# mLSTM kernel: q and k transposed by TensorE in four tiles and scored in fp32

## The chip, the cores and the metric

The kernel runs on one core of one Trainium2 chip. A core has TensorE (matrix products, shown as PE, its loads of the stationary operand as PEld), VectorE (DVE), ScalarE (ACT), GpSimd (POOL) and SyncE (SP), which here only issues DMAs. The metric is device time in microseconds (us) of one execution; a kernel's time is the median of its runs.

## What is computed

Four batches, eight heads, 768 steps, head dimension 40, all in fp32: a gated linear attention (mLSTM) with a running maximum, then a gated layer with a causal convolution of five taps.

```python
for t in range(S):
    m_new = np.maximum(f_gate[:, :, t] + m, i_gate[:, :, t])
    f_stab = np.exp(f_gate[:, :, t] + m - m_new)
    i_stab = np.exp(i_gate[:, :, t] - m_new)
    m = m_new
    C = f_stab[:, :, None, None] * C + i_stab[:, :, None, None] * np.einsum('bhd,bhe->bhde', vt, kt)
    n = f_stab[:, :, None] * n + i_stab[:, :, None] * kt
    h_tilde = np.einsum('bhde,bhe->bhd', C, qt)
    nq = np.einsum('bhd,bhd->bh', n, qt)[:, :, None]
    denom = np.maximum(np.abs(nq), 1.0)
    y[:, :, t] = o * h_tilde / denom
...
# x is y with the heads side by side: (4, 768, 320)
gate = 1.0 / (1.0 + np.exp(-gate_pre))      # gate_pre: causal convolution of x over 5 steps
val = x @ w_val
return (gate * val @ w_out)
```

## The kernel before

Time is cut into six stretches j of 128 steps, each stretch into two chunks p of 64. A *unit* u = 4j + b is one stretch of one batch b with all eight heads; a *group* g = 2u + p is one chunk of it. There are 24 units and 48 groups. Within a group the recurrence is done as masked attention over 64 steps, with the state of the chunk before as 40 more rows of the key side.

Per group: `args` (L353, psd) makes the logarithms of the decays with one bf16 matmul, `expo` (L366, dm) takes their exponential on ScalarE, `scores` (L371, pss) multiplies k with q, `probs` (L387, pt) multiplies scores and decays on VectorE, `keyw` (L396, kw) weighs the keys on POOL, `state` (L410, pc) and `state_out` carry the state, `heads` (L435, ph) multiplies pt with the values and the state in vc. Per unit `norm`, `norm_o`, `gate_o` make x, `x_tr` (px) transposes it, and `x_copy`, `x_rest` put it into xc and x3. After each stretch the layer runs on x: `conv0`, `conv`, `conv3` (sg, pg), `sigmoid`, `val` (pf), `z_mul` and its parts, `outp` (po), `outp_st`, `out_dma`.

For `scores` q and k are needed with the 40 columns on the partitions. Before, each block of 128x320 is turned in five steps: `prep_max` (L286, ScalarE) finds each row's largest value, `prep_scale` (L290, VectorE) makes a power of two from it (scl, and cmp for undoing it), `prep_hi` (L318, POOL) writes the scaled fp16 upper half into stk, `prep_lo` (L324, VectorE) the lower half and a second copy of one half, and `prep_tr` (L340) has a DMA transpose it into tq (q) or tk (k). One score matmul with 3 x 40 = 120 rows then sums the three products of halves. Its stationary side tk also holds identity columns (`idk`), so that the same matmul leaves q itself in the state rows. The scale of k is undone in `probs`, that of q in `norm` by the lower bound of the denominator (sct; from j = 1 on made by `scale_mul` and `scale_out`, since q is loaded there with its steps in another order). k also goes from nat into kp, where chunk 0 stands in the upper and chunk 1 in the lower 64 partitions (`load_k`), by a DMA except at the very start.

Three things set the order. The start is written out by hand (L689 to L778). After it each piece of work has a due time in units of groups, from the table LAGS and the loops at its end (`at`), and is emitted in that order; a scheduler then orders each engine's instructions by simulated time. SyncE's queue, which issues nearly all DMAs, keeps the written order. One pool of five PSUM buffers of 2 KB per partition (`ps_s`, NSH = 5, tag "big") goes round among psd, pss, px, pg, pf and po: each new tile takes the buffer of the fifth before it and waits until that one has been read. Of the start: the gates of the first stretch are computed by `gates(0, P)` on VectorE, sent through DRAM by `spread_out` and `spread_in`, and come back as rows of la and ra, without which no `args` can run; `gates(P, S)` does the other five stretches.

Of the kernel before, what the change touches and what calls it, by code (L numbers as in the profile page):

```python
# [88 lines left out]
def tile_mlstm_gated_ffn(  # L89
# [65 lines left out]
    nat = [cst.tile([P, 2, BH, D], F32, name=f"nat{i}") for i in range(2)]  # L155
    kp = cst.tile([P, 2, BH, D], F32, name="kp")
# [16 lines left out]
    tk_ = [cst.tile([P, L + H * (P + L)], F16, name=f"tk{i}") for i in range(3)]  # L173
    cmp_ = [cst.tile([P, 2, B], F32, name=f"cmp{i}") for i in range(2)]
    sct = [cst.tile([P, B], F32, name=f"sct{i}") for i in range(2)]
    spg = cst.tile([P, PB, R], BF16, name="spg")
    sel_g = cst.tile([P, PB], F32, name="sel_g")
    sel_b = cst.tile([P, B], BF16, name="sel_b")
    scl = [cst.tile([P, 2, B], F32, name=f"scl{i}") for i in range(2)]
    amx = [cst.tile([P, 2, B], F32, name=f"amx{i}") for i in range(2)]  # L180
    stk = [cst.tile([P, 2, H, P], F16, name=f"stk{i}") for i in range(2)]


    def load_qk(j, x, b0, b1):
        ts = slice(j * P, (j + 1) * P)
        if x == 1 or j == 0:
            hs = slice(b0 * H, b1 * H)
            nc.sync.dma_start(nat[j % 2][:, x, hs], (qv, kv)[x][ts, hs])
            return
        dst = nat[j % 2][:, 0].rearrange("p (h r) d -> p h (r d)", r=R)  # L190
        for b in range(b0, b1):
            nc.sync.dma_start(dst[b * PB : (b + 1) * PB], q[b, :, ts].rearrange("h (g r) d -> g h (r d)", r=R))

    def load_k(j, p, i):
        hs = slice(i * BH // 2, (i + 1) * BH // 2)
        put = nc.scalar.copy if j == i == 0 else nc.vector.tensor_copy if j < T["kpe"] else nc.sync.dma_start
        put(kp[TOK[p] : TOK[p] + L, p, hs], nat[j % 2][p * L : (p + 1) * L, 1, hs])
# [80 lines left out]
    MASKE = 0x7F800000  # L278

    def part(j, x, i):  # L280
        src = nat[j % 2][:, x]
# [4 lines left out]
    def prep_max(j, i, x):  # L286
        junk = wk.tile([P, H, D], BF16, name=f"junk{j}_{i}_{x}", tag="junk", bufs=1)
        nc.scalar.activation(junk, part(j, x, i), AF.Abs, accum_out=amx[j % 2][:, x, i : i + 1])  # L288
# [29 lines left out]
    def prep_hi(j, i, x):  # L318
        o, v, f = stk[i % 2][:, x, :, 0:D], part(j, x, i), scl[j % 2][:, x, i : i + 1]
        if j > 0 and turn("on_act_hi", 2 * i + x):  # L320
            return nc.scalar.activation(o, v, AF.Copy, scale=f)
# [618 lines left out]
```

## Time and profile before

| | |
|---|---|
| median of three runs | 292.95 us |
| the three runs | 294.02, 292.95, 290.55 us |
| the profiled execution | 292.77 us |
| its span in the profile | 291.0 us |
| mean granted clock of TensorE | 0.871 |

A line of a profile names an engine, a line of the kernel (L441), the operation and the tiles, written as output<-inputs without their numbers. In the group rows the figures after the bar are the busy time of all instances, the mean in ns of one, and the idle time just before them with what ended it. In the windows each engine's busy time in a stretch of the span stands with its number of instructions, then the granted clock as a share of full speed, the DMA share and GB/s. In the timeline and the chain the first column is the start in us from the beginning of the span, the second the duration; instructions of the same line in a row are merged. Matmuls are pipelined: the durations of neighbours overlap, and their starts tell the pace. An fp32 matmul shows as two records, each with its own load of the stationary operand, unless it is a transpose by the transpose operation (px). A few matmul records can be missing.

### The profile page before, as it was taken

How to read it: one execution, taken by the hardware profiler on the slowest of the kernel's cores; microseconds unless marked ns; L12 is line 12 of the kernel's file. 1: busy time of each engine (PE TensorE's matmuls, PEld its weight loads, DVE VectorE, ACT ScalarE, POOL GpSimd, SP SyncE). 2: the span in 40 equal slices, each digit the busy share in tenths (PEclk: the TensorE clock that was granted, in tenths of full speed). 3: DMA queues.
4: the chain of work that ended last, by engine and by line, in shares of the span. 5: the costliest groups of instructions: out<-in, count | busy, mean ns of one | idle time of the engine just before them, and what ended most of it. 6: DMA issues, size and time to landing. Idle time of an engine off the chain costs nothing.

```text
span 291.0 us, 6696 instructions
## 1 busy us (share of the span) xinstructions
PE 226.1 (78%) x2411; PEld 186.5 (64%) x2411; DVE 224.3 (77%) x526; ACT 155.1 (53%) x354; POOL 176.5 (61%) x276
## 2 busy tenths in 40 slices
PE   0045736915945879997699996997999999999985
PEld 0034536715834758775588674886779977887974
DVE  7999995844799999879999535999569852883940
ACT  4267352362982744696812189633495446435262
POOL 7565534623999566897973536783479451954541
PEclk9999555685997675999958995999999999999999
DMA  7899699999999999998908999901999630010112
GB/s 138 150 146 169 109 200 159 198 184 125 198 165 222 194 179 161 170 214 135 122 2 157 193 211 198 113 2 38 198 213 153 168 62 2 0 66 27 45 47 90
DMA packets 145897, 38.73 MB, mean 133 GB/s; under 512 B 135176, under 2 KB 143752, under 8 KB 145864
## 3 DMA queue, kind: packets, MB, share of 16 engines
q1 hardware_dynamic: 143044, 37.76, 79.8%
q10 hardware_dynamic: 2820, 0.54, 1.1%
q8 instruction: 19, 0.31, 0.5%
q14 instruction: 14, 0.11, 0.1%
HBM read 17.87 MB, written 4.23 MB: 76 GB/s over the span
## 4 chain that ended last, share of the span: by engine, by line
PE 41%; DVE 30%; DMA 10%; issue 8%; ACT 4%; SPq 3%; POOL 3%; ACTq 0%; POOLq 0%; DVEq 0%
PE ph L441 12%; PE pf L545 7%; DVE sg L510 7%; PE pc L418 5%; PE pss L384 5%; PE po L571 4%; DVE stk L327 3%; DVE stk L336 3%; DMA tq<-stk 3%; PE pg L522 3%; DVE pt L391 3%; PE psd L357 3%; PE px L479 2%; DMA out_dram<-ob 2%; DMA kp<-nat 2%
## 5 line engine op out<-in xcount | busy, mean ns | idle before, releaser
L441 PE MATMUL ph<-vc,pt 128*64 128x41 f32 (+1 forms) x768 | 61.3, 248 | 19.4 <-DVE x L470 12.5
L441 PEld LDWEIGHTS ph<-vc,pt 128*64 128x64 f32 (+1 forms) x768 | 55.4, 156 | 32.1 <-DVE x L470 15.6
L322 POOL TENSOR_SCALAR stk<-nat,scl 128x320 f16<-128x320 f32 x48 | 32.3, 677 | 42.0 <-DMA tq<-stk 13.5
L418 PE MATMUL pc<-vc,kw 128*40 128x41 f32 (+1 forms) x704 | 43.8, 226 | 12.0 <-POOL kw L403 4.7
L418 PEld LDWEIGHTS pc<-vc,kw 128*40 128x40 f32 (+1 forms) x704 | 37.6, 138 | 18.0 <-POOL stk L322 7.6
L510 DVE SCALAR_TENSOR_TENSOR sg<-xc,cwt,sg 128x512 f32<-128x512 f32 (+1 forms) x56 | 45.9, 846 | 1.4 <-POOL sg L504 1.2
L403 POOL TENSOR_TENSOR kw<-kp,dm 128x320 f32<-128x320 f32 (+1 forms) x44 | 37.1, 846 | 10.3 <-DMA kp<-nat 3.9
L391 DVE SCALAR_TENSOR_TENSOR pt<-pss,cmp,dm 128x512 f32<-128x512 f32 x48 | 35.4, 738 | 9.8 <-PE pss L384 5.6
L327 DVE SCALAR_TENSOR_TENSOR stk<-nat,scl,stk 128x320 f16<-128x320 f32 x48 | 35.8, 746 | 6.8 <-POOL stk L322 6.6
L368 ACT ACTIVATE dm<-psd 128x512 f32<-128x512 f32 x48 | 28.4, 597 | 22.5 <-POOL kw L403 7.0
L357 PE MATMUL psd<-ra,la 120*128 120x512 bf16 x48 | 21.9, 457 | 20.7 <-DMA la<-gda 18.5
L384 PE MATMUL pss<-tq,tk 120*128 120x64 f16 x384 | 33.2, 259 | 3.1 <-DVE pt L391 1.7
L384 PEld LDWEIGHTS <-tk 120*128 120x128 f16 x384 | 26.7, 128 | 9.8 <-issue 5.8
L288 ACT ACTIVATE junk<-nat 128x320 bf16<-128x320 f32 x48 | 22.5, 470 | 18.9 <-DMA nat<-in_q_dram 9.4
L431 ACT COPY vc<-pc 40x328 f32<-40x328 f32 x44 | 18.7, 426 | 25.6 <-PE pc L418 23.7
L495 POOL TENSOR_TENSOR xl<-xc,xh 128x256 fp32r<-128x256 f32 x24 | 18.6, 776 | 17.7 <-ACT xc L488 17.7
L465 POOL TENSOR_TENSOR rs<-sg,den 128x320 f32<-128x320 f32 x24 | 19.6, 817 | 10.4 <-DVE den L460 8.6
L550 DVE TENSOR_TENSOR sg<-pf,sg 128x512 f32<-128x512 f32 (+3 forms) x21 | 12.5, 609 | 15.6 <-ACT sg L530 11.4
L559 POOL TENSOR_TENSOR zl<-sg,zh 128x512 fp32r<-128x512 f32 (+1 forms) x14 | 15.8, 1135 | 13.7 <-ACT zh L554 13.6
L571 PE MATMUL po<-woh,zh 128*128 128x320 f32 x72 | 21.5, 345 | 2.6 <-DVE pt L391 2.6
L576 ACT COPY ob<-po 128x320 f32<-128x320 f32 x24 | 9.6, 426 | 25.4 <-PE po L571 14.8
L336 DVE COPY stk<-stk 128x320 f16<-128x320 f16 x48 | 20.2, 421 | 0.0
(150 smaller groups left out, 451.2 us busy)
## 6 DMA issues: line engine op xcount, KB each, us to landing
nat<-in_q_dram SPq DMA_DIRECT2D x24, 160.0 KB, 4.0
vc<-in_v_dram SPq DMA_DIRECT2D x12, 320.0 KB, 5.0
sg<-in_o_gate_dram SPq DMA_DIRECT2D x6, 640.0 KB, 5.6
out_dram<-ob SPq DMA_DIRECT2D x24, 160.0 KB, 2.1
kp<-nat SPq DMA_DIRECT2D x22, 160.0 KB, 3.3
nat<-in_k_dram SPq DMA_DIRECT2D x10, 320.0 KB, 5.5
nat<-in_k_dram SPq DMA_DIRECT2D x4, 160.0 KB, 3.4
rawv<-in_moe_w_val_dram SPq DMA_DIRECT2D x4, 160.0 KB, 3.7
```

The source lines that it names most:

```text
L322: return nc.gpsimd.tensor_scalar(o, v, f, 1.0, op0=ALU.mult, op1=ALU.mult)
L327: nc.vector.scalar_tensor_tensor(t[:, :, lo : lo + D], part(j, x, i), scl[j % 2][:, x, i : i + 1], t[:, :, 0:D], op0=ALU.mult, op1=ALU.sub ...
L336: return put(t[:, :, dup : dup + D], t[:, :, 0:D])
L357: nc.tensor.matmul(psd, la[:, p, j, b], ra[:, :, j], start=True, stop=True,)
L368: nc.scalar.activation(dm, psd_[g], AF.Exp)
L384: nc.tensor.matmul(o, tk[h], tq[:, h], start=True, stop=True)
L391: nc.vector.scalar_tensor_tensor(pt, pss_[g], cmp_[j % 2][:, p, b : b + 1], dmt[g], op0=ALU.mult, op1=ALU.mult)
L403: (nc.vector if turn("on_dve_kw", b) else nc.gpsimd).tensor_mul(kw[0:n], kp[0:n, p, b * H : (b + 1) * H], dmt[g][0:n, :, L - 1 : L].to_bro ...
L418: nc.tensor.matmul(pc[n0 : n0 + D, h], kwt[g][0 : ROWS[p], h], vc[j % 2][0 : ROWS[p], p, b * H + h], start=True, stop=True)
L441: nc.tensor.matmul(pht[u][p * L : (p + 1) * L, h], ptt[g][0 : ROWS[p], h], vc[j % 2][0 : ROWS[p], p, b * H + h], start=True, stop=True,)
L510: nc.vector.scalar_tensor_tensor(o, xc[j % 2][:, c, b0:b1, t : t + P], cwt[:, c, t : t + 1], o, op0=ALU.mult, op1=ALU.add)
L571: nc.tensor.matmul(pf, z, w, start=(i == 0), stop=(i == len(mm) - 1))
```

## The change

The whole preparation of halves goes: `prep_max`, `prep_scale`, `prep_hi`, `prep_lo`, `prep_tr`, `scale_mul`, `scale_out`, `idk`, and the tiles stk, tk, tq, scl, amx, cmp, sct. k is loaded by DMA straight into kp, of which there are two now (by j % 2), so the copies from nat to kp go as well; q is loaded in its natural order. Each kp has its constant part (identity and zeros), written by POOL.

`tr(u)` turns a unit's q and k with 32 fp32 matmuls against the identity. Rows 0 to 63 and 64 to 127 of the source (r) and two halves of the output partitions (i) address four quarters of TensorE's array. The results stand in two PSUM tiles pT, copied to SBUF by `tr_out`. `scores(u)` makes both groups of a unit at once: 16 fp32 matmuls of 40 rows, again in four quarters, and four against the identity that put q into the state rows, into two PSUM tiles (still named pss), even heads in one and odd heads in the other. `probs` therefore runs in two halves, and no scale is undone. The lower bound of the denominator is 1 again. At the start the four units of j = 0 are turned before anything else, unit 0's scores are written by hand, the copies of ra and la for the other stretches come right behind the gates, and `spread_out(1)` and `spread_in(1)` go through SyncE's queue.

```diff
-    nat = [cst.tile([P, 2, BH, D], F32, name=f"nat{i}") for i in range(2)]
-    kp = cst.tile([P, 2, BH, D], F32, name="kp")
+    nat = [cst.tile([P, BH, D], F32, name=f"nat{i}") for i in range(2)]
+    kp = [cst.tile([P, 2, BH, D], F32, name=f"kp{i}") for i in range(2)]
...
+    def load_k(j, p, b0, b1):
+        hs = slice(b0 * H, b1 * H)
+        c = slice(j * P + p * L, j * P + (p + 1) * L)
+        nc.sync.dma_start(kp[j % 2][TOK[p] : TOK[p] + L, p, hs], kv[c, hs])
...
-    def prep_max(j, i, x):
-        junk = wk.tile([P, H, D], BF16, name=f"junk{j}_{i}_{x}", tag="junk", bufs=1)
-        nc.scalar.activation(junk, part(j, x, i), AF.Abs, accum_out=amx[j % 2][:, x, i : i + 1])
...
-        nc.sync.dma_start_transpose(t, stk[i % 2][:, x].rearrange("p h n -> p (h n)"))
...
+    def tr(u):
+        j, b = divmod(u, B)
+        pT = [ps_s.tile([P, 2, H // 2, L], F32, name=f"pT{u}_{r}", tag="big") for r in range(2)]
+        kf = kp[j % 2].rearrange("p x n d -> p (x n d)")
+        qf = nat[j % 2].rearrange("p n d -> p (n d)")
+        with tc.manual_schedule(engines={mybir.EngineType.PE}):
+            for h in range(0, H, 2):
+                for x in range(2):
+                    for r in range(2):
+                        rows = slice(r * L, (r + 1) * L)
+                        for i, m in ((0, L), (1, D)):
+                            c = (b * H + h + i) * D + (x * (1 - r)) * BH * D
+                            nc.tensor.matmul(
+                                pT[r][i * L : i * L + m, x, h // 2],
+                                (qf, kf)[x][rows, c : c + m],
+                                ident[rows, rows],
+                                start=True,
+                                stop=True,
+                            )
+        qk_ps[u] = pT
+
+    def tr_out(u, r):
+        t = wk.tile([P, 2, H // 2, L], F32, name=f"qk{u}_{r}", tag=f"qk{r}", bufs=4)
+        (nc.scalar.copy if r == 0 or u < B else nc.vector.tensor_copy)(t[0:NT], qk_ps[u][r][0:NT])
+        qk_[u, r] = t
+
+    def scores(u):
+        eo = [ps_s.tile([P, 2, H // 2, L], F32, name=f"pss{u}_{i}", tag="big") for i in range(2)]
+        q = [qk_[u, p][:, 0] for p in range(2)]
+        k = [qk_[u, 1 - p][:, 1] for p in range(2)]
+        rows = [slice(i * L, i * L + D) for i in range(2)]
+
+        with tc.manual_schedule(engines={mybir.EngineType.PE}):
+            for h in range(H // 2):
+                for p in range(2):
+                    for i, r in enumerate(rows):
+                        o = eo[i][TOK[p] : TOK[p] + L, p, h]
+                        nc.tensor.matmul(o, k[p][r, h], q[p][r, h], start=True, stop=True)
+            for p in range(2):
+                for i, r in enumerate(rows):
+                    o = eo[i][STA[p] : STA[p] + L, p]
+                    nc.tensor.matmul(o, ident[r, i * L : (i + 1) * L], q[p][r], start=True, stop=True)
...
-        nc.vector.scalar_tensor_tensor(
-            pt, pss_[g], cmp_[j % 2][:, p, b : b + 1], dmt[g], op0=ALU.mult, op1=ALU.mult
-        )
+        po, do = (t.rearrange("k (h i) l -> k i h l", i=2) for t in (pt, dmt[g]))
+        for i in range(2):
+            nc.vector.tensor_mul(po[:, i], pss_[u][i][:, p], do[:, i])
...
-            nc.vector.tensor_scalar(dnt[u], nq, -1.0, sct[j % 2][:, b : b + 1], op0=ALU.mult, op1=ALU.max)
+            nc.vector.tensor_scalar(dnt[u], nq, -1.0, 1.0, op0=ALU.mult, op1=ALU.max)
...
+        if u >= B:
+            at(t - 4.7, tr, u)
+            for r in range(2):
+                at(t - 4.4, tr_out, u, r)
+        if u > 0:
+            at(t + lag("scores", j), scores, u)
```

TensorE's queue around a unit in the second stretch, before. The number behind a name tells tiles apart; pss is one group's scores, and its matmul (L384) stands eight times in a row with a load of tk before each, of which the last is shown:

```order
L384 LDWEIGHTS tk_102
L384 MATMUL pss_1680<-tq_956,tk_102 128x4x16
L441 MATMUL ph_1639<-vc_84,pt_1586 64x41 x8
L545 MATMUL pf_2_0_1690<-xh_600,wvh 64x512 x2
L418 MATMUL pc_1671<-vc_84,kw_1477 40x41 x8
```

The same engine after, around unit 5's values (ph_1155), unit 7's transposes (pT) and, further on, unit 6's scores (pss_0, pss_1):

```order
L362 MATMUL pc_1085<-vc_86,kw_926 40x41 x8
L317 LDWEIGHTS la
L317 MATMUL psd_1101<-ra,la 128x512
L423 MATMUL px_1111<-ident,x_924 128x128 x2
L423 MATMUL px_1111<-ident,x_924 64x128
L276 MATMUL pT_0_1118<-ident,nat_82 64x64
L276 MATMUL pT_0_1118<-ident,nat_82 40x64
L385 MATMUL ph_1155<-vc_86,pt_1098 64x41 x3
L276 MATMUL pT_1_1119<-ident,nat_82 64x64
L276 MATMUL pT_1_1119<-ident,nat_82 40x64
L276 MATMUL pT_0_1118<-ident,kp_84 64x64
L276 MATMUL pT_0_1118<-ident,kp_84 40x64
```

Where a group's eight scores stood, a unit's 32 transposes and its 20 score matmuls stand now; each quarter of the array gets one instruction, then the next quarter.

SyncE's queue around the load of the third stretch, before (stk to tq and tk are the transposes, nat to kp the copies of k):

```order
L347 DMA_TRANSPOSE tq_485<-stk_115 128x8x128
L197 DMA kp_83<-nat_82 64x640
L192 DMA nat_81<-in_q_dram 32x8x160 x4
L188 DMA nat_81<-in_k_dram 128x16x40
L347 DMA_TRANSPOSE tk_101<-stk_114 128x8x128
L347 DMA_TRANSPOSE tq_485<-stk_114 128x8x128
```

and after, from the gates' way through DRAM (gsp, gdg, gda) on:

```order
L240 DMA gdg_110<-gsp_108 32x6x320
L245 DMA gda_112<-gsp_108 240x1x64 x4
L174 DMA nat_82<-in_q_dram 128x32x40
L179 DMA kp_84<-in_k_dram 64x16x40 x2
L252 DMA ra<-gdg_110 24x8x320
L254 DMA la<-gda_112 24x20x64 x2
```

No transposes and no copies are left in that queue, and the gates of the later stretches go through it.

VectorE's queue before, where the convolution (L510) of the second stretch begins (amx belongs to the scales, pt is `probs`, den `norm`):

```order
L510 SCALAR_TENSOR_TENSOR sg<-xc_90,cwt,sg 128x512 x2
L293 TENSOR_SCALAR amx_112<-amx_112 128x4
L391 SCALAR_TENSOR_TENSOR pt_1837<-pss_1796,cmp_104,dm_1731 128x512
L510 SCALAR_TENSOR_TENSOR sg<-xc_90,cwt,sg 128x512
L294 TENSOR_SCALAR amx_112<-amx_112 128x4
```

and after, at the first stretch's convolution (L454; x_92 is `x_rest`, qk the copy out of PSUM):

```order
L438 TENSOR_TENSOR x_92<-px_1263,x_92 64x128
L454 SCALAR_TENSOR_TENSOR sg<-xc_90,cwt,sg 128x512 x8
L287 COPY qk_1_1337<-pT_1_1271 104x512
L337 TENSOR_TENSOR pt_1403<-pss_0_1347,dm_1261 128x4x64
L337 TENSOR_TENSOR pt_1403<-pss_1_1348,dm_1261 128x4x64
```

The eight instructions of the convolution stand in one piece there, ahead of the copy and of `probs`.

More of the change, by code (lines that the diff above doesn't have):

```diff
@@ L172, in tile_mlstm_gated_ffn, with load_q @@
     cwt = cst.tile([P, 3, 5], F32, name="cwt")
[L173 to L197, printed above, removed]
+    def load_q(j, b0, b1):
+        hs = slice(b0 * H, b1 * H)
+        nc.sync.dma_start(nat[j % 2][:, hs], qv[j * P : (j + 1) * P, hs])
+    def load_k(j, p, b0, b1):
+        hs = slice(b0 * H, b1 * H)
+        c = slice(j * P + p * L, j * P + (p + 1) * L)
+        nc.sync.dma_start(kp[j % 2][TOK[p] : TOK[p] + L, p, hs], kv[c, hs])
     def load_v(j, p):
@@ L308, in scale_mul @@
-    def scale_mul(j):
-        nc.vector.tensor_mul(
-            spg, sel_g[:, :, None].to_broadcast([P, PB, R]), scl[j % 2][:, 0, None, :].to_broadcast([P, PB, R])
-        )
-    def scale_out(j):
-        pq = ps_s.tile([P, B], F32, name=f"pq{j}", tag="big")
-        nc.tensor.matmul(pq, spg.rearrange("p g r -> p (g r)"), sel_b, start=True, stop=True)
-        nc.vector.tensor_copy(sct[j % 2], pq)
[L318 to L321, printed above, removed]
-        return nc.gpsimd.tensor_scalar(o, v, f, 1.0, op0=ALU.mult, op1=ALU.mult)
@@ L699, in tile_mlstm_gated_ffn @@
         nc.vector.memset(tl, 0.0)
-        nc.vector.memset(tr, 0.0)
+        nc.vector.memset(tr0, 0.0)
         for x in range(3):
@@ L769, in tile_mlstm_gated_ffn @@
-        nc.vector.tensor_copy(sct[0], scl[0][:, 0])
-        run(rest)
-        spread_out(1, nc.scalar.dma_start)
-        for i in range(2):
-            load_qk(1, 1, 2 * i, 2 * i + 2)
-        nc.gpsimd.memset(gt[L:P, 2], 0.0)
-        i4 = ident.rearrange("p (b g) -> p b g", b=B)
-        with nc.allow_low_precision("one of each sum is 1, the others 0"):
-            nc.vector.tensor_reduce(sel_b, i4, axis=AX.X, op=ALU.add)
-        nc.vector.tensor_reduce(sel_g, i4.rearrange("p b g -> p g b"), axis=AX.X, op=ALU.add)
@@ L780, in consts1 @@
-    def consts1():
-        for j in range(1, NJ):
-            yield nc.vector.tensor_copy(ra[:, :, j], tr)
-            yield nc.vector.tensor_copy(la[:, :, j], tl)
+        for g in range(2):
+            args(g)
+        scores(0)
+        for g in range(2):
+            expo(g)
+            keyw(g)
+        for _ in range(6):
+            next(rest)
+        for g in range(2):
+            probs(g)
+        sig_o(0)
+        run(rest)
+        spread_out(1, nc.sync.dma_start)
+        *_, last_dve = consts1()
@@ L785, in consts2 @@
+        load_q(1, 0, B)
+        for p in range(2):
+            load_k(1, p, 0, 2)
+        spread_in(1, nc.sync.dma_start)
+        for p in range(2):
+            load_k(1, p, 2, 4)
     def consts2():
@@ L787, in consts2 @@
             yield vc_const(1, p)
+        for p in range(2):
+            yield kp_const(1, p)
+        nc.gpsimd.memset(gt[L:P, 2], 0.0)
         nc.gpsimd.memset(xc[0][:, :, :, 0:4], 0.0)
```

208 lines of the change are left out of this document (42 added, 166 removed).

## The prediction

> **What bounds the kernel now.** I read the page first (sections 1, 2 and 4), then the windows view cut where the stages change, then the chain of waits, the group rows and a piece of TensorE's timeline.
>
> ```profile
> span 291.0 us, 6696 instructions
> PE 226.1 (78%) x2411; PEld 186.5 (64%) x2411; DVE 224.3 (77%) x526; ACT 155.1 (53%) x354; POOL 176.5 (61%) x276
> PEclk9999555685997675999958995999999999999999
> DMA  7899699999999999998908999901999630010112
> PE 41%; DVE 30%; DMA 10%; issue 8%; ACT 4%; SPq 3%; POOL 3%; ACTq 0%; POOLq 0%; DVEq 0%
> ```
>
> No engine fills the span: TensorE and VectorE are both at 77 to 78%, and the DMA line shows the queues full for two thirds of it. The first value matmul of unit 0 starts at 22.7 us, that of unit 4 (the first of j = 1) at 73.4, of unit 16 (j = 4) at 200.3, and the last value work ends at 257.3. Cut at these places:
>
> ```profile
> core 0: us, PE busy (x) PEld busy (x) DVE busy (x) ACT busy (x) POOL busy (x), PEclk, DMA share, GB/s
> 0.00:22.70 22.70, 3.46 (x35) 2.42 (x35) 20.13 (x59) 10.48 (x23) 14.18 (x35) 1.00 0.90 148
> 22.70:73.40 50.70, 29.77 (x360) 25.15 (x360) 38.01 (x112) 23.75 (x63) 23.14 (x37) 0.63 1.10 162
> 73.40:200.30 126.90, 106.91 (x1184) 86.66 (x1181) 108.69 (x243) 75.68 (x175) 90.75 (x136) 0.85 0.95 152
> 200.30:257.30 57.00, 57.00 (x648) 46.56 (x648) 40.38 (x83) 30.05 (x60) 35.13 (x52) 1.00 0.60 102
> 257.30:291.00 33.70, 28.98 (x189) 25.76 (x189) 17.05 (x36) 15.15 (x36) 13.34 (x17) 1.00 0.17 60
> ```
>
> The kernel has three regimes. From 22.7 to 73.4 TensorE works 29.77 of 50.7 us at a granted clock of 0.63 while the DMA share is over 1. From 73.4 to 200.3 TensorE (84% of the stretch) and VectorE (86%) limit each other. From 200.3 to 257.3 TensorE is busy all the time at full clock: there it alone is the bound. What holds the first regime is a transfer:
>
> ```profile
> 61.48 4.96 DMA kp<-nat
> 66.44 3.21 DMA tq<-stk
> 69.70 1.04 PE pss L384 x8
> ...
> SPq L347 <- DVE stk L336: 36.2, 7, 11.6
> ```
>
> The copy of k to its place and a transpose of q end just before the score matmuls that wait for them, and the one SP queue stood 36.2 us in all behind VectorE's halves.
>
> **What the change removes.** Each of the 48 blocks of q or k loses these rows, and the small scale instructions around them:
>
> ```profile
> L327 DVE SCALAR_TENSOR_TENSOR stk<-nat,scl,stk 128x320 f16<-128x320 f32 x48 | 35.8, 746 | 6.8 <-POOL stk L322 6.6
> L336 DVE COPY stk<-stk 128x320 f16<-128x320 f16 x48 | 20.2, 421 | 0.0
> L322 POOL TENSOR_SCALAR stk<-nat,scl 128x320 f16<-128x320 f32 x48 | 32.3, 677 | 42.0 <-DMA tq<-stk 13.5 <-DMA tk<-stk 8.8 <-DMA nat<-in_k_dram 8.0
> L288 ACT ACTIVATE junk<-nat 128x320 bf16<-128x320 f32 x48 | 22.5, 470 | 18.9 <-DMA nat<-in_q_dram 9.4 <-DMA nat<-in_k_dram 4.2 <-issue 3.6
> ```
>
> That is at least 56 us of VectorE, 32 of POOL and 22 of ScalarE, and all DMA transposes and copies of k on SP. From TensorE it takes the old scores:
>
> ```profile
> 22.70:73.40 50.70, 5.86 (x72) 5.87 (x9) 0.63 1.10 162
> 73.40:200.30 126.90, 18.56 (x203) 18.48 (x25) 0.85 0.95 152
> 200.30:257.30 57.00, 7.56 (x96) 10.34 (x14) 1.00 0.60 102
> ```
>
> (the windows of the tile pss, TensorE first).
>
> **What it adds on the vector engines.** Two copies of 128x512 out of PSUM per unit, 28 on ScalarE and 20 on VectorE, and `probs` in two halves. The nearest rows:
>
> ```profile
> L368 ACT ACTIVATE dm<-psd 128x512 f32<-128x512 f32 x48 | 28.4, 597 | 22.5 <-POOL kw L403 7.0 <-PE psd L357 5.7 <-DVE pt L391 3.4
> L550 DVE TENSOR_TENSOR sg<-pf,sg 128x512 f32<-128x512 f32 x10 | 6.8, 689 | 10.6 <-ACT sg L530 8.8 <-PE pf L545 1.7
> L550 DVE TENSOR_TENSOR sg<-pf,sg 128x256 f32<-128x256 f32 x4 | 1.6, 422 | 2.7 <-ACT sg L530 2.6 <-PE pf L545 0.2
> L510 DVE SCALAR_TENSOR_TENSOR sg<-xc,cwt,sg 128x512 f32<-128x512 f32 x40 | 37.2, 943 | 0.2
> ```
>
> ScalarE gets 28 x 0.60 = 17 us, VectorE 20 x 0.69 = 14 us and 96 x 0.42 us of `probs` where 48 x 0.74 stood (5 us more). Both end lighter than before (VectorE near 185 us or less), so I cost these at nothing; their cover is TensorE's own work in the same stretch. POOL's four constant copies into kp stand in the first 22.7 us or beside unit 0; I cost them at nothing too.
>
> **What it adds on TensorE.** Each unit gets 32 transposing matmuls (64 or 40 columns stationary, 64 moving) and 20 score matmuls (16 with 64 moving columns, 4 with 256), all fp32 on quarters of the array. The rows that price them:
>
> ```profile
> 218.04 0.69 PE L418 MATMUL pc<-vc,kw 104*40 104x41 f32 x13
> 218.54 0.25 PE L441 MATMUL ph<-vc,pt 104*64 104x41 f32 x1
> 218.58 0.24 PE L418 MATMUL pc<-vc,kw 104*40 104x41 f32 x2
> 218.62 0.23 PE L441 MATMUL ph<-vc,pt 104*64 104x41 f32 x1
> 218.65 0.20 PE L418 MATMUL pc<-vc,kw 104*40 104x41 f32 x1
> 218.68 0.99 PE L441 MATMUL ph<-vc,pt 104*64 104x41 f32 x14
> 219.60 0.62 PE L384 MATMUL pss<-tq,tk 120*128 120x64 f16 x8
> 220.03 0.41 PE L357 MATMUL psd<-ra,la 120*128 120x512 bf16 x1
> 220.37 1.12 PE L441 MATMUL ph<-vc,pt 128*64 128x41 f32 x16
> 221.42 0.55 PE L479 MATMUL px<-ident,x 128*128 128x128 f32 x3
> 221.81 0.39 PE L384 MATMUL pss<-tq,tk 120*128 120x64 f16 x4
> ```
>
> First, an fp32 matmul of eight heads shows as 16 records, so each counts twice. Second, 14 records of ph last 0.99 us, and a single one 0.23: they start (0.99 - 0.23)/13 = 58 ns apart. Three px records with 128 moving columns take 221.81 - 221.42 = 0.39, 0.13 each, so 256 columns cost between 0.13 and 0.26; I take 0.24, since twice the columns stream. Third, pc and ph lie in different column halves, and ph starts while the last three records of pc's 16 have not started; both then keep their own pace. Tiles of the array do run side by side, and the engine reaches over some four records to start another tile. In the new order each instruction puts two records on one tile and the next two on another, so four records reach into three tiles. That rows of the array also run apart no row here shows. The bounds are a depth n of 4 (all quarters) and of 1 (nothing overlaps); n = 3 is nearest to what the rows above show.
>
> Per unit alone: transposes 64 x 0.058 = 3.71 us, scores 32 x 0.058 + 8 x 0.24 = 3.78 us; divided by n = 3, 1.24 and 1.26.
>
> The transposes of units 0 to 3 stand at the start, where TensorE has 3.46 us of work in 22.7: hidden, even at half clock (4 x 1.24 x 2 = 10 us).
>
> **The sum.**
> - Start, 22.7: kept. The gate work and its way through DRAM stay, and set the first score of the old kernel too.
> - 22.7 to 73.4: TensorE's 29.77, less 5.86, plus transposes of units 4 and 5 and scores of 1 to 4, (7.42 + 15.12)/3 at a clock of about 0.75 (between 0.63 and 1) = 10.0: 33.9 instead of 50.7. The bound from above is 50.7, if something other than those transfers holds it.
> - 73.4 to 257.3 (183.9): TensorE now. The second regime's 106.91 would be between 106.91 x 0.85 = 91 and 107 at full clock; I take 97, and 57.0 for the third: 154. Less 299 old score records at (220.03 - 219.60)/8 = 54 ns: 16. Plus 18 transposes and 19 scores, (66.8 + 71.8)/3 = 46.2. The waits for switching between array forms (219.60 after ph's last start, about 0.1 us) stay equal in number. 184.2. For waits I add 7: VectorE now has eight convolution instructions of 943 ns in a row once (j = 0) and up to four later, with `probs` behind them, and TensorE waits for `probs`; 7.5 us, mostly.
> - Tail 33.7: kept. Outside the span 292.77 - 291.0 = 1.8.
>
> 22.7 + 33.9 + 184.2 + 7 + 33.7 + 1.8 = **283.3 us, say 283**. The profiled execution took 292.77, the median of the runs is 292.95, so no correction. The gain is 17 us in the first regime; the third loses some 13, the second wins some 5.
>
> In the depth n the time is 283 + (138.6 + 30)(1/n - 1/3): 269 at n = 4, 311 at n = 2, 396 at n = 1. It breaks even with 293 at n = 2.6. This margin is thin, and it decides.
>
> **Rivals.**
> - *Two quarters at a time, 311 us (slower).* For it: every overlap in the trace is of two column halves with all rows; none shows two row halves. Against: the depth in records would allow three. It decides from n = 2.6 down, at TensorE, in 73.4 to 257.3.
> - *Starts are limited, 302 us.* Between 218.54 and 218.68 five records start: 28 ns apart, and no denser stretch lasts. Were that a floor for all tiles together, the 64-column records (64 x 18 + 32 x 19 = 1760 of them) would cost 28 instead of 19.3: 15.3 more, and 3 in the first regime. Against: those gaps are explained by the two tiles' own paces. The Trainium skill, "TensorE: Matmul & The Clock Gate", section "Wait — 56ns, not 53.3ns?", states a floor of about 25 ns between starts however small the matmul; by it the sum would be 295, within a per cent of no change. The shortest gaps here (0.01 to 0.04 us between rows of pc and ph) neither hold nor break an average of 25.
> - *VectorE's blocks stall TensorE, about 296 us.* The five PSUM buffers go round: a transpose's second tile takes the buffer of the scores two units earlier, free only after both `probs`. If each of five feeds delayed `probs` by 4 us, 20 instead of 7. Against: VectorE is lighter than before in every stretch.
> - *The first regime does not shrink, 300 us.* If the clock of 0.63 or VectorE's gate work, not the transfers, held it.
> - *Nothing overlaps, 396 us*: the quarters would not do what they are for.
>
> **Numbers.** A measurement of this kernel tells about 1% from no change. Overlap of 2.7 to 4 deep, my forecast: 0.52, with its own range of 269 to 290. Limited starts 0.16, two quarters 0.13, VectorE's blocks 0.09, first regime kept 0.06, nothing overlaps 0.02, still faster than 268 (depth 4 and no waits) 0.02. Under 290.0 lie 0.49 of the first and the last: 0.51. Between 290 and 295.9 lie 0.03 of the first, 0.06 of limited starts and 0.05 of the blocks: 0.14. Slower: 0.35. The range 268 to 306 leaves out two quarters, no overlap and the fastest: 0.17.
>
> **What would show it.** The group of the transposes (tile pT): its busy time per 64 records, 1.2 us if right, 1.9 for two quarters, 3.7 for none. Value matmuls of unit 4 near 57 us, and a PEclk near 1 from there on. TensorE busy over 90% between there and the last value matmul. No waits for a DMA in front of scores. I am wrong if pT takes over 1.5 us per unit, if TensorE waits often for pt or for a PSUM buffer, or if unit 4 still starts after 65 us.

## The result, and the profile after

| | before | after |
|---|---|---|
| median | 292.98 us (4 runs, 290.55 to 294.02) | 332.06 us (4 runs, 329.96 to 335.8) |
| profiled execution, its span | 292.77, 291.0 us | 331.63, 329.6 us |
| ratio after to before | | 1.132 (95%: 1.122 to 1.143) |

The change costs 39 us. The forecast was 283, with 268 to 306 as its range: wrong in sign and out of its range. (Ratios here and below leave out disturbed executions, in which either kernel is a few per cent longer; medians hold every execution, so the two can differ.)

The page of the changed kernel, the lines that answer to the first five of the prediction:

```profile
span 329.6 us, 10471 instructions
PE 271.6 (82%) x4518; PEld 217.3 (66%) x4518; DVE 175.9 (53%) x388; ACT 142.7 (43%) x282; POOL 146.5 (44%) x230
PEclk9975566577677596999969999999998999999999
DMA  7892999607929000698114791057400110002022
PE 38%; DVE 27%; POOL 8%; SPq 7%; ACT 7%; DMA 7%; issue 6%; ACTq 0%; DVEq 0%; POOLq 0%
```

VectorE, ScalarE and POOL all have less to do than before (VectorE 175.9 us instead of 224.3), and the DMA line is far from full. Still 27% of the chain that ended last runs over VectorE, an engine that is idle for half of the span. The largest single part of it, 12% of the span, is the taps of the convolution (sg L454); the rest is many small steps. So having little work has not kept the engine off the chain, and what stands in its queue, and when, is what to look for next. The windows, cut at the first value matmul of unit 0, 4 and 16 and at the last value work, as in the prediction:

```profile
0.00:23.50 23.50, 11.56 (x327) 9.19 (x327) 20.09 (x26) 7.94 (x12) 19.80 (x39) 0.94 0.79 112
23.50:76.30 52.80, 38.78 (x534) 30.68 (x534) 24.93 (x70) 18.65 (x33) 18.38 (x32) 0.56 0.72 98
76.30:222.70 146.40, 120.25 (x2280) 95.60 (x2278) 76.16 (x171) 66.06 (x134) 63.84 (x96) 0.86 0.49 73
222.70:295.60 72.90, 71.64 (x1187) 55.74 (x1187) 37.33 (x86) 34.91 (x68) 29.98 (x46) 0.98 0.16 31
295.60:329.60 34.00, 29.39 (x198) 26.05 (x196) 17.38 (x37) 15.14 (x36) 14.50 (x18) 1.00 0.17 59
```

(Columns as in the prediction.) Start and tail are as forecast, 23.5 and 34.0 for 22.7 and 33.7. The first regime, 23.5 to 76.3, was to take 33.9 and takes 52.8: 18.9 too many. From 76.3 to 295.6 it was to be 191.2 and is 219.3: 28.1 too many. TensorE works 191.9 us there where 184.2 were forecast (7.7 more) and is idle for 27.4 where 7 were (20.4 more); 26 of the idle time lies between 76.3 and 222.7. These two sums are the whole miss of 48 us, with some 1 us at the two ends.

**TensorE's price per unit was right, in part by luck.** The windows of the tile pT and then of pss, TensorE first, from unit 16 on, and the start and end of one unit's transposes at full clock:

```profile
222.70:295.60 72.90, 7.22 (x320) 6.21 (x320) 3.40 (x5) 2.92 (x5) 0.98 0.16 31
222.70:295.60 72.90, 7.91 (x280) 4.72 (x280) 10.48 (x28) 0.98 0.16 31
218.05 0.34 PE L276 MATMUL pT<-ident,nat 64*64 64x64 f32 x8
218.20 0.30 PE L276 MATMUL pT<-ident,kp 64*40 64x64 f32 x8
...
218.87 0.22 PE L276 MATMUL pT<-ident,kp 64*40 64x64 f32 x1
...
218.88 0.32 PE L276 MATMUL pT<-ident,kp 64*40 64x64 f32 x7
```

Five units of transposes take 7.22 us, 1.44 each; seven of scores 7.91, 1.13 each; together 2.57 where I had 1.24 + 1.26 = 2.50. In a row the 64 transposing records start within 218.05 and about 218.98 (the last row's end less one record's 0.22), 15 ns apart, against the 58 ns of ph's records on one tile before. That is a depth of four (58 / 15 = 3.9), not my three; the rest of the 1.44 is latency at the ends. So 1.24 for the transposes was too little and 1.26 for the scores too much, and the sum agrees because the two errors cancel. The rivals of two quarters, of limited starts and of no overlap are out. As a floor for all four quarters together, the about 25 ns between starts that the Trainium skill gives ("TensorE: Matmul & The Clock Gate", section "Wait — 56ns, not 53.3ns?") is out too: the rows differ from it, and they decide.

**Where TensorE waits.** Of the waits of the whole span the longest of TensorE and one of VectorE, then rows of TensorE's, of VectorE's and of SyncE's timeline (in brackets the idle time just before, and what ended it):

```profile
PE ph L385 <- DVE pt L337: 22.3, 7, 10.2
...
DVE ca_vo L533 <- DMA rawvo<-in_moe_w_out_dram: 7.5, 1, 7.5
```

```profile
52.83 0.59 PE L317 MATMUL psd<-ra,la 120*128 120x512 bf16 x1 [4.10 <-ACT qk L287]
61.20 1.61 PE L385 MATMUL ph<-vc,pt 128*64 128x41 f32 x15 [7.10 <-DVE pt L337]
109.90 1.62 PE L385 MATMUL ph<-vc,pt 128*64 128x41 f32 x12 [10.23 <-DVE pt L337]
123.23 0.90 PE L423 MATMUL px<-ident,x 128*128 128x128 f32 x3 [4.44 <-DVE qk L287]
```

```profile
50.96 0.17 DVE L533 TENSOR_SCALAR ca_c<-rawc 128x15 int32<-128x15 int32 x1 [5.73 <-DMA rawc<-in_moe_conv_w_dram]
60.48 0.33 DVE L533 TENSOR_SCALAR ca_v<-rawv 128x320 int32<-128x320 int32 x1 [7.34 <-DMA rawv<-in_moe_w_val_dram]
87.12 0.33 DVE L533 TENSOR_SCALAR ca_vo<-rawvo 128x320 int32<-128x320 int32 x1 [7.50 <-DMA rawvo<-in_moe_w_out_dram]
103.52 0.33 DVE L533 TENSOR_SCALAR ca_o<-rawo 128x320 int32<-128x320 int32 x1 [5.81 <-DMA rawo<-in_moe_w_out_dram]
115.33 7.24 DVE L454 SCALAR_TENSOR_TENSOR sg<-xc,cwt,sg 128x512 f32<-128x512 f32 x8 [0.69 <-POOL sg L448]
```

```profile
43.54 3.05 SPq L582 DMA_DIRECT2D rawc<-in_moe_conv_w_dram  x2
52.69 5.71 SPq L556 DMA_DIRECT2D rawv<-in_moe_w_val_dram  x4
```

The weights of the layer come in as float64 (the raw tiles) and are turned into fp32 by `f64_to_f32`: six steps on VectorE with one on POOL and one on ScalarE between them, for the taps (c) and five tiles of 128x320. VectorE works its queue in order. It stands 26.4 us in all before four raw loads (5.73 + 7.34 + 7.50 + 5.81), and twice the `probs` of the unit in hand come only behind such a load: TensorE idles 7.10 us for them at 61.20 and 10.23 at 109.90. At 123.23 it idles 4.44 us for a copy of pT (qk) that stands behind the block of eight taps. In the kernel before, the same loads cost VectorE 1.42 and 1.71 us, and the other two nothing:

```profile
62.82 1.29 SPq L638 DMA_DIRECT2D rawc<-in_moe_conv_w_dram  x2
68.12 0.17 DVE L589 TENSOR_SCALAR ca_c<-rawc 128x15 int32<-128x15 int32 x1 [1.42 <-DMA rawc<-in_moe_conv_w_dram]
77.53 0.37 DVE L589 TENSOR_SCALAR ca_v<-rawv 128x320 int32<-128x320 int32 x1 [1.71 <-DMA rawv<-in_moe_w_val_dram]
```

There VectorE had the halves to make in the meantime. Without them it reaches the conversion at 50.96 instead of 68.12, and the load of the taps, issued at 43.54 instead of 62.82, has not landed.

### The profile page after: what moved, and what is told of

Its sections match the earlier page's. It is cut to its first block, busy times and chain, and to the rows that moved or that the text cites. A ratio compares the mean times of both kernels' runs of the same rounds, so it can differ in the third digit from the quotient of the medians.

```text
span 329.6 us, 10471 instructions
## 1 busy us (share of the span) xinstructions
PE 271.6 (82%) x4518; PEld 217.3 (66%) x4518; DVE 175.9 (53%) x388; ACT 142.7 (43%) x282; POOL 146.5 (44%) x230
## 4 chain that ended last, share of the span: by engine, by line
PE 38%; DVE 27%; POOL 8%; SPq 7%; ACT 7%; DMA 7%; issue 6%; ACTq 0%; DVEq 0%; POOLq 0%
DVE sg L454 12%; PE ph L385 8%; PE pT L276 6%; PE po L515 5%; PE pg L466 4%; PE pc L362 4%; PE pf L489 3%; ACT sg L474 2%; SPq L179 2%; PE pss L303 2%; PE psd L317 2%; DVE pt L337 2%; PE px L423 2%; DMA out_dram<-ob 2%; DMA rawvo<-in_moe_w_out_dram 2%
## 5 line engine op out<-in xcount | busy, mean ns | idle before, releaser
L385 PE MATMUL ph<-vc,pt 104*64 104x41 f32 (+1 forms) x768 | 67.9, 254 | 29.2 <-DVE pt L337 22.3
L385 PEld LDWEIGHTS ph<-vc,pt 104*64 104x64 f32 (+1 forms) x768 | 59.5, 161 | 42.5 <-DVE pt L337 22.4
L454 DVE SCALAR_TENSOR_TENSOR sg<-xc,cwt,sg 128x512 f32<-128x512 f32 (+1 forms) x56 | 48.9, 903 | 8.6 <-POOL sg L448 8.2
L337 DVE TENSOR_TENSOR pt<-pss,dm 128x256 f32<-128x256 f32 x96 | 35.8, 414 | 28.6 <-PE pss L307 23.8
L276 PE MATMUL pT<-ident,nat 64*40 64x64 f32 (+1 forms) x768 | 38.0, 268 | 8.3 <-DMA nat<-in_q_dram 4.7
L276 PEld LDWEIGHTS pT<-ident,nat 64*64 64x64 f32 (+1 forms) x768 | 31.6, 161 | 13.4 <-POOL tl L607 4.4
L276 PE MATMUL pT<-ident,kp 64*64 64x64 f32 (+1 forms) x768 | 34.7, 265 | 4.3 <-DMA kp<-in_k_dram 4.3
L276 PEld LDWEIGHTS pT<-ident,kp 64*64 64x64 f32 (+1 forms) x768 | 30.8, 162 | 4.9 <-DMA kp<-in_k_dram 4.9
L375 ACT COPY vc<-pc 40x328 f32<-40x328 f32 x44 | 18.7, 425 | 33.9 <-PE pc L362 33.1
L287 ACT COPY qk<-pT 104x512 f32<-104x512 f32 x28 | 15.9, 584 | 25.4 <-PE pT L276 19.8
L494 DVE TENSOR_TENSOR sg<-pf,sg 128x512 f32<-128x512 f32 (+3 forms) x21 | 12.6, 608 | 22.7 <-ACT sg L474 16.6
L303 PE MATMUL pss<-qk,qk 40*64 40x64 f32 x768 | 21.2, 241 | 0.7 <-DVE x L438 0.7
L303 PEld LDWEIGHTS pss<-qk,qk 40*64 40x64 f32 x768 | 16.7, 149 | 6.9 <-issue 2.1
```

Of the source, the lines that this page charges most:

```text
L276: nc.tensor.matmul(pT[r][i * L : i * L + m, x, h // 2], (qf, kf)[x][rows, c : c + m], ident[rows, rows], start=True, stop=True,)
L303: nc.tensor.matmul(o, k[p][r, h], q[p][r, h], start=True, stop=True)
L337: nc.vector.tensor_mul(po[:, i], pss_[u][i][:, p], do[:, i])
L375: put(dst[n0 : n0 + D, b * H : (b + 1) * H], pct[g][n0 : n0 + D])
L385: nc.tensor.matmul(pht[u][p * L : (p + 1) * L, h], ptt[g][0 : ROWS[p], h], vc[j % 2][0 : ROWS[p], p, b * H + h], start=True, stop=True,)
L454: nc.vector.scalar_tensor_tensor(o, xc[j % 2][:, c, b0:b1, t : t + P], cwt[:, c, t : t + 1], o, op0=ALU.mult, op1=ALU.add)
```

## The experiments

Theory W, after this reading: the wait for late weights costs some 26 us, TensorE's work the rest. Theory P: the transposes themselves cost it. The late weights turned out to be only the first layer.

**1. Weights fetched ahead.** All raw loads are issued right behind `load_o(0)` in the start, with five raw buffers instead of two:

```diff
         load_o(0)
+        fetch()
```

> The changed kernel, but all loads of the raw weights stand in SyncE's queue right behind the first load of o_gate, into five buffers instead of two, ahead of the gates' second way through DRAM. Theory W (VectorE stands still for the late weights, 5.7 + 7.3 + 7.5 + 5.8 = 26 us in the trace, with probs behind it): 332 falls by 20 to 30, to 302 to 312, and VectorE's waits for rawc, rawv, rawvo, rawo are gone. Theory P (TensorE's added transposes and scores are the whole price): the waits turn into TensorE's own work, 325 or more.

Measured: 318.2 us median of 5; ratio 1.070 (1.052 to 1.089), which on 292.98 is 313.6. That is 18 us less than the changed kernel by the ratio and just outside W's interval. W has a part; but in the profiled execution, the longest of the five (335.3 us), unit 4 still begins at 76.2, so the first regime has not moved. VectorE waits for no raw load any more, and TensorE still waits 9.4 us in one piece for `probs`.

(Numbers are those of the labels; there is no 10.)

**2. No transposes from unit 4 on**; the scores reuse the turned q and k of the first stretch:

```diff
-        q = [qk_[u, p][:, 0] for p in range(2)]
-        k = [qk_[u, 1 - p][:, 1] for p in range(2)]
+        q = [qk_[u % B, p][:, 0] for p in range(2)]
+        k = [qk_[u % B, 1 - p][:, 1] for p in range(2)]
...
-        if u >= B:
-            at(t - 4.7, tr, u)
-            for r in range(2):
-                at(t - 4.4, tr_out, u, r)
```

> The changed kernel without the transposes and their copies from the second stretch on: the scores of all later units use the q and k of the first stretch (the output is another). TensorE loses 20 of 24 units' transposes, 29 us busy in the second and third regimes. Theory W: the weights' waits stay and hide most of it, 332 falls by 7 to 17, to 315 to 325. Theory P: it falls by the whole 29 or more, to 303 or less.

Measured: 315.0 in one run, at the lower end of what W expected and 12 above P's. With every transpose beyond the start gone the kernel is still 20 us slower than before. VectorE still stands 19.7 us before the four raw loads. Unit 4 begins at 68.5 instead of 76.3, though only two units' transposes lie ahead of it; with the queues in order this difference is gone (67.0 and 68.5 in experiments 11 and 12).

**3. Both.**

> Both edits: weights loaded ahead, and no transposes after the first stretch (the output is another). Theory W: with the waits gone TensorE's work is the bound, so the transposes now cost what they take: 18 to 28 under the first run's time, 278 to 290. Theory P: about the time without transposes, 300.

Measured: 306.3 in one run, neither's number, though nearer to P's 300. The window from unit 4 on shows why this run decides nothing:

```profile
68.90:129.00 60.10, 59.74 (x646) 45.52 (x644) 23.11 (x66) 18.61 (x41) 21.91 (x36) 0.50 0.72 89
```

TensorE is busy for 59.74 of 60.10 us, at a granted clock of 0.50. The run says nothing against W, nor for it.

**4. Weights ahead, and the eight taps of the first stretch spread over more due time** (0.327 to 1.6; some taps then come behind the sigmoid, which changes the output):

> Weights loaded ahead, and the first stretch's eight convolution instructions are due further apart, so that four and four stand together on VectorE instead of eight. If the block of eight (7.2 us) held probs: 2 to 4 us less than with the weights ahead alone. If not: the same within 1 us.

Measured: 312.1 median of 4, 1.064 (1.050 to 1.077): 2 us less than experiment 1 by the ratios, within the uncertainty of both, so the block of eight is not decided by it. Its profile is of more use. This table holds it and the ones that follow with their transposes, cut at the first value matmuls of units 0, 4 and 12 (read off TensorE's timeline), with TensorE's busy time and granted clock in the middle part; from unit 12 on the clock was 1.00 in experiments 7, 11 and 12, where it was read. Each row is one execution; that of experiment 11 is its longest (308.7 us), that of 13 too (296.6).

| us | unit 0 to 4 | 4 to 12 | TensorE busy there, clock | 12 to the end |
|---|---|---|---|---|
| before | 50.7 | 75.6 | 60.6, 0.84 | 141.9 |
| after | 52.7 | 97.2 | 74.1, 0.80 | 156.0 |
| 4, weights ahead, taps due later | 51.7 | 74.7 | 66.0, 0.91 | 158.6 |
| 5, and o_gate load earlier | 50.0 | 81.8 | 69.9, 0.85 | 155.5 |
| 6, q and k of stretch 1 early | 53.2 | 80.4 | 68.6, 0.87 | 156.3 |
| 7, paced | 51.3 | 84.8 | 72.8, 0.82 | 149.4 |
| 8, conversion left out | 48.8 | 79.4 | 67.5, 0.89 | 156.7 |
| 9, paced, o_gate load earlier | 44.2 | 90.9 | 78.6, 0.76 | 149.3 |
| 11, paced, all loads in order | 43.8 | 90.3 | 78.9, 0.75 | 149.4 |
| 13, and the sigmoid paced | 34.6 | 86.9 | 85.2, 0.69 | 149.4 |

Between units 4 and 12 the same 1390 or so matmul records take TensorE 66 us at a clock of 0.91 and 85 at 0.69, so that column is to be read with its clock: busy time times clock is 59 to 60 us in every row with the change. TensorE's idle time there is 23 us in the changed kernel (97.2 - 74.1) and 9 in experiment 4: the weights' waits are gone. The first regime stays.

**5. The o_gate load of stretch 1 earlier.** In experiment 4 ScalarE stands before the sigmoid of that tile, whose load SyncE issues at 54.77, behind loads of k for stretch 2 that hold its queue from 50.36 on. One number of the due times moves it ahead of them, and the taps are due 0.8 apart (all before the sigmoid):

```diff
-"og1": 4.264
+"og1": 0
```

> The weights are fetched ahead as in the first experiment, the eight convolution taps of the first stretch are due 0.8 apart (all ahead of the sigmoid), and the o_gate load of stretch 1 is issued ahead of the loads of q and k for stretch 2, where it stood behind them. Theory S (the first stretch is held by the order in SyncE's queue: loads stand behind a wait for k's readers, sigmoid and score products wait for the o_gate load): 300 to 307 us, first value matmul of unit 4 at 66 to 70 us instead of about 75. Theory V (the first stretch is held by the vector engines' own in-order work on gates and weights, the loads are late because of it): 309 to 314, unit 4 at 73 or later.

Measured: 312.6 median of 4, 1.070 (1.061 to 1.078); unit 4 at 73.9. V's numbers. The sigmoid does come 8.7 us earlier than in experiment 4 (52.82 for 61.52), and the next exp only 1.7 earlier (64.27 for 65.95), because now the conversion stands in between.

**6. q and k of stretch 1 right behind those of stretch 0** as well, weights behind the spreading of the gates:

```diff
         load_o(0)
+        fetch_taps()
+        load_q(1, 0, B)
+        for i in range(2):
+            for p in range(2):
+                load_k(1, p, 2 * i, 2 * i + 2)
...
         spread_out(1, nc.sync.dma_start)
+        fetch()
```

> As the one before, and q and k of stretch 1 are loaded right behind the loads of stretch 0 (SyncE issues them at about 20 to 28 us, when it stood idle waiting for the gates), the other weights behind the spreading of the gates, and the conversion of the weights is due 1.6 half-units later. Theory S: unit 4's first value matmul at 58 to 66 us and 288 to 299 us in all. Theory V: unit 4 at 72 or later and 305 us or more. In both the second half (unit 12 to the end) keeps its 156 to 159 us, since TensorE alone bounds it.

Measured: 318.5 median of 4, 1.082 (1.076 to 1.088), unit 4 at 76.9. S fails here, but the run does not test it cleanly: pushing the weights back brought VectorE's wait back, [7.22 <-DMA rawv] at 42.33.

**7. Pacing.** Theory V now: with the loads early, the scheduler puts the whole conversion between units 1 and 4, since its inputs are ready and VectorE idle. Here each conversion step and each tap is queued behind the last `probs`, `expo` or `keyw` written before it, so that the written order holds (`issue_after` fixes the order within one engine's queue):

```diff
+            tail["dve"] = nc.vector.tensor_mul(po[:, i], pss_[u][i][:, p], do[:, i]).ins
...
+        with tc.issue_after(tail["dve"]):
             nc.vector.scalar_tensor_tensor(
...
+    def paced(it):
+        with tc.issue_after(tail["dve"]), tc.issue_after(tail["act"]), tc.issue_after(tail["pool"]):
+            for _ in range(2):
+                next(it, None)
```

> The weights are fetched ahead, and every step of their conversion and every convolution tap is queued behind the last probs, exp and key weighting that was written before it, so that the order of the code, not readiness, sets where they stand in VectorE's, ScalarE's and POOL's queues. Theory V (in-order queues: once the loads are early, the conversion of all five weight tiles stands between units 1 and 4 and holds the score products of the first stretch behind its hops from engine to engine): unit 4's first value matmul at 58 to 66 us instead of 74 to 76, no VectorE block of taps over 3 us, 290 to 301 us in all. Rival T (TensorE's own transposes and scores fill that stretch): unit 4 at 72 or later, 306 or more.

Measured: 310.6 median of 4, 1.063 (1.053 to 1.074), unit 4 at 74.4. V misses and T's numbers hold, but not T's reason: TensorE works only 35 of these 51 us. The last column of the table fell by 6 to 9 us and stays there in all paced kernels; that late only taps are left to pace (the last step of a conversion starts at 136.40, unit 12 at 159.2), and the taps' share of the chain, 12% of the span in the changed kernel, is 2%.

**8. Conversion left out.** One copy of the high words takes its place, nothing is paced.

> The weights are fetched ahead, and their conversion from float64 is left out: one VectorE copy of the high words takes its place (the output is another one); nothing is paced. Theory V: unit 4 at 56 to 66 us, and 290 to 300 us. Theory T: unit 4 at 72 or later, 306 or more.

Measured: 310.9 in one run, unit 4 at 73.0. Conversion alone does not hold the first regime. What does, in this kernel, stands in ScalarE's timeline and in the waits between 22 and 78 us:

```profile
50.24 1.28 ACT L477 ACT_TABLE_LOAD   x1
61.66 1.27 ACT L477 ACTIVATE sg<-sg 128x1280 f32<-128x1280 f32 x1 [10.14 <-DMA sg<-in_o_gate_dram]
62.96 0.43 ACT L375 COPY vc<-pc 40x328 f32<-40x328 f32 x1
```

```profile
PE ph L385 <- ACT vc L375: 10.5, 1, 10.5
```

ScalarE stands 10.14 us before the sigmoid of the o_gate of stretch 1. That sigmoid is needed only in unit 4, but the copy of a state that TensorE needs now is behind it, and TensorE waits 10.5 us for it. In experiment 7 ScalarE stands 10.75 us before the same sigmoid.

**9. Paced, and the o_gate load earlier.**

> As the paced kernel, and the o_gate load of stretch 1 is issued ahead of the loads of q and k of stretch 2. If the sigmoid of stretch 1 waits for that load in the paced kernel, this gives another 3 to 7 us; if TensorE or the score products hold the first stretch there, nothing within 2 us.

Measured: 311.2 median of 4, 1.068 (1.063 to 1.074): the time did not change. The first regime did: unit 4 at 67.8 instead of 74.4. So four kernels stand together: neither the earlier load (5: 73.9) nor removing the conversion from the way (7: 74.4; 8: 73.0) frees unit 4, both do (67.8). Two covers lay one behind the other, and taking away one shows the other. The 6.6 us are given back by unit 12 (90.9 for 84.8), not to a new wait: TensorE idles 12 us there in both, and works 78.6 instead of 72.8 us, at a clock of 0.76 instead of 0.82. Each number is of one execution, but the medians, 311.2 and 310.6, agree with them.

**11. All loads of stretch 1 first, paced.** q, k and o_gate of stretch 1 behind the loads of stretch 0, then the gates spread, the taps, the gates read back, the other weights; the conversion due one half-unit later.

```diff
         load_o(0)
+        load_q(1, 0, B)
+        for i in range(2):
+            for p in range(2):
+                load_k(1, p, 2 * i, 2 * i + 2)
+        load_o(1)
...
+        fetch_taps()
         spread_in(1, nc.sync.dma_start)
+        fetch()
```

> The paced kernel with a new order in SyncE's queue: q, k and o_gate of stretch 1 are loaded right behind the loads of stretch 0, then the gates are spread, then the taps, the gates are read back, and then the other weights. Theory Q (the first stretch was held by two covers, one behind the other: the conversion of the weights in the in-order queues, and where it was gone, ScalarE standing 10 to 12 us before the o_gate load with the copies of the states behind it): unit 4 at 54 to 62 us, 290 to 299 us in all. Theory T (TensorE's own 35 us and the hops between the engines hold it, the loads were never last): unit 4 at 66 or later, 303 or more.

Measured: 301.4 median of 4, 1.030 (1.015 to 1.044): 10 us less than experiment 9, short of Q's interval. Unit 4 at 67.0. ScalarE's and TensorE's rows name the rest:

```profile
38.75 1.27 ACT L479 ACTIVATE sg<-sg 128x1280 f32<-128x1280 f32 x1 [7.14 <-DMA sg<-in_o_gate_dram]
40.04 0.43 ACT L376 COPY vc<-pc 40x328 f32<-40x328 f32 x1
```

```profile
40.52 1.61 PE L386 MATMUL ph<-vc,pt 104*64 104x41 f32 x13 [9.17 <-ACT vc L376]
```

With its load early the scheduler has moved the sigmoid itself forward, before the first copy of a state: the same wait, 23 us earlier.

**12. The same without transposes from unit 4 on**, as in 2.

> The same without the transposes and their copies from unit 4 on (the scores reuse the transposed q and k of stretch 0, so the output is another one). With the loads and the pacing in order TensorE is the bound from unit 4 on, so 20 units of transposes should show at their full price: by my price of 1.24 us a unit and the measured 1.36 of busy time a unit, 18 to 27 us less than the kernel above; if they lay beside other work, under 10 us less.

Measured: 288.9 median of 10, 0.982 (0.976 to 0.988). The two ratios differ by 0.048, 13.9 us on 292.1, for 20 units: 0.70 each, below the expectation and above its rival. The two intervals leave room for 8 to 20 us, so neither is excluded. From unit 12 to the end, at full clock in both, ten units of transposes make 149.4 - 140.0 = 9.4 us: 0.94 each, of 1.28 busy (12.8 us for 640 records). A part does lie beside other work.

**13. The sigmoid paced too.**

```diff
+        with tc.issue_after(tail["act"]):
             nc.scalar.activation(og[j % 2], og[j % 2], AF.Sigmoid)
```

> The kernel with pacing and all loads in order, and the sigmoid of the o_gate of stretches 1 and 2 is also queued behind the exp written before it (in that kernel it stood ahead of the first copy of a state and made ScalarE wait 7.1 us for its load, and TensorE 9.2 us for the copy). Theory Q (queue order, cover behind cover): unit 4's first value matmul at 55 to 61 us instead of 67, and 289 to 296 us. Theory T (what is left in the first stretch is TensorE and the hops): unit 4 at 65 or later and 299 or more.

Measured: 291.3 median of 7 (285.2 to 296.6) beside 293.3 of the kernel before; ratio 0.978 (0.970 to 0.986), which rests on the two shortest, 285.2 and 286.8. Unit 4 at 58.2. Q holds in every number, and this is a kernel with the change that is no slower than the one without it: by the medians 0.993, by the ratio faster. Its page and its windows, cut as above without the cut at unit 16 (the profiled execution is the one of 296.6):

```profile
PE 274.3 (93%) x4518; PEld 218.6 (74%) x4518; DVE 170.1 (58%) x388; ACT 142.7 (48%) x282; POOL 146.1 (50%) x230
...
PE 79%; DVE 4%; SPq 2%; DMA 1%; ACT 1%; issue 1%; ACTq 0%; DVEq 0%
```

```profile
0.00:23.60 23.60, 12.84 (x328) 9.72 (x328) 20.31 (x28) 8.05 (x12) 19.93 (x38) 1.00 0.76 110
23.60:58.20 34.60, 32.03 (x536) 25.43 (x535) 20.54 (x60) 13.72 (x28) 10.63 (x18) 1.00 0.96 150
58.20:260.50 202.30, 200.63 (x3471) 157.88 (x3471) 110.98 (x265) 106.41 (x209) 100.82 (x158) 0.87 0.43 64
260.50:294.50 34.00, 28.81 (x190) 25.52 (x188) 18.32 (x37) 14.51 (x33) 14.69 (x18) 1.00 0.17 59
```

VectorE is off the chain (4%, from 27%), and TensorE is busy 32.0 of 34.6 us in the first regime and 200.6 of 202.3 after it. (The clock of 1.00 in the first two windows is not to be trusted; the last section shows why.) The work is that of the changed kernel, to the instruction on the four engines: 4518, 388, 282 and 230. Only the order in the queues, and three more raw buffers, differ.

## Why the prediction was wrong

- **"Both end lighter than before, so I cost these at nothing; their cover is TensorE's own work."** This step failed. That the engines are lighter is true (175.9 for 224.3 us); that lighter means hidden is not, where an engine works in order. What counts is who stands first in the queue and when its input comes. VectorE, freed of the halves, reached the weights before their loads: 26.4 us of waiting in four places, with TensorE idle behind them (7.10, 10.23). The added copies of pT were not hidden either where they stood behind other work: TensorE idled 4.10 and 4.44 us for two of them. I had named `probs` as queued behind the taps, and did not ask what else it was queued behind.
- **"First regime: 33.9 instead of 50.7."** The size was right and the condition missing. The transfers that held it did go, but behind them lay the weights, behind the weights the sigmoid waiting for o_gate. Experiments 5, 7, 8, 9, 11 and 13 took these away one after the other, and at the end it measured 34.6. I had called 50.7 the bound "if something other than those transfers holds it", and gave that 0.06, thinking of the clock or the gates only; the clock alone did not hold it, for in experiment 13 TensorE's rows keep to the same half pace until some 46 us and unit 4 still starts at 58.2. Of the 18.2 us between 52.8 and 34.6, 11.4 are TensorE's idle time (14.0 to 2.6 us), which the queues made; 6.8 are its busy time (38.8 to 32.0), the same work at a faster pace.
- **"For waits I add 7."** Between 76.3 and 295.6 TensorE is idle for 27.4 us. The term was mis-sized by the same step. The block of eight taps was as foreseen (7.24 us, with TensorE idle for 4.44 of it); pacing the taps is worth 6 to 9 us, but from unit 12 on.
- **TensorE's work, 184.2 us, and the depth on which I thought the outcome hung:** 2.57 for 2.50 us a unit is right, with the luck of two errors that cancel; 191.9 us were worked, at a clock of 0.86 from 76.3 to 222.7 and 0.98 after. In experiment 13 the stretch of 191.2 takes 202.3, with TensorE busy all through, at a clock of 0.69 between units 4 and 12; at experiment 4's 0.91 its work there would be 19 us shorter (66.0 for 85.2), by estimate.
- **The start, the tail, no DMA wait before scores:** as foreseen. "Unit 4 near 57" came true only in experiment 13 (58.2). Of the signs that I was wrong two came: TensorE waits for pt (22.3 us), and unit 4 starts at 76.3, after 65.
- **Rivals:** "VectorE's blocks stall TensorE, 296" named the right engine, with chance 0.09, but at 13 us of the 48 that were missing; "the first regime does not shrink" came true as well. Both at once was not among the cases, though one cause feeds both.

What is settled: order alone gives the 39 us back, since the same instructions in another order take 285 to 297. How the 39 us divide among the layers isn't, as they hide one another: the earlier o_gate load adds nothing to the total on top of experiment 1 (experiment 5) or of experiment 7 (experiment 9). The pacing of the taps was never tried without that of the conversion, so their shares stay open too. Not tried either: the same pacing in the kernel before, so how much of 13's gain the change could claim for itself is open.

## What to carry to other kernels

When a change takes work off an engine, ask of each engine that it frees what stands next in its queue and whether that instruction's input will be there so much earlier; a wait there is charged to everyone behind it. Read "off the critical path" as a statement on the old order only. When removing one wait changes nothing, look at what the same engine or the next now waits for before giving up the theory: here only the second and third removal, together with the first, showed the gain.

## What was not expected of the hardware

The granted clock halves under full work, and took back part of what order gained. These are the windows from 84 to 124 us of experiment 4 and then of experiment 13:

```profile
84.00:124.00 40.00, 37.97 (x885) 30.85 (x886) 21.07 (x57) 20.06 (x45) 17.58 (x26) 0.90 0.64 84
84.00:124.00 40.00, 40.00 (x536) 30.84 (x535) 23.55 (x55) 14.54 (x33) 18.30 (x25) 0.50 0.53 68
```

TensorE is busy for 40 of 40 us at 0.50 and gets 536 records done, where another kernel at 0.90 does 885. Experiment 3 held 0.50 through 60 us of unbroken work. So a low clock is no sign here that TensorE lacks work, and being busy does not bring it back. In the table the clock between units 4 and 12 is lowest where TensorE idles least (1.7 us in experiment 13) but 0.91 at 9 us of idle time and 0.82 at 12, so idle time does not decide it either; what does, no run here shows.

The clock that a view prints can also be no reading at all. These are two rows of experiment 13, 13 records of one shape each, in places where its windows print 1.00:

```profile
31.02 1.61 PE L386 MATMUL ph<-vc,pt 104*64 104x41 f32 x13
54.20 0.95 PE L386 MATMUL ph<-vc,pt 104*64 104x41 f32 x13
```

The first runs at the pace that the changed kernel has at a printed clock of 0.50 (1.61 us at 30.34), the second at that of full clock. In experiment 13 the rows keep to the slow pace until some 46 us. So it is in experiment 4, where its first regime prints 0.83: 14 records of ph take 1.71 us at 34.65, as in the changed kernel at 34.08. Busy time times clock shows it as well: for nearly the same records of the first regime it is 21.7 us in the changed kernel (38.8 at 0.56) and 20.1 in experiment 11 (33.0 at 0.61), but 30.6 in experiment 4 (36.8 at 0.83) and 32.0 in experiment 13. Where the clock bears on an argument, check it against the starts of the rows.

Last, four quarters of the array run fully side by side in fp32: the 64 starts of a unit's transposes take 0.93 us, 15 ns for each, where ph's records on one tile take 58.
